# VectorE transposes in an attention and S4 kernel: reciprocals and maxima moved off TensorE, last two units normalised by halves, third quarter of wo moved forward, u times D moved to VectorE

## The chip, the core and the metric

The kernel runs on one core of a Trainium2 chip. The metric is the device time of one launch in microseconds, the median of several executions. Beside the timed runs stands one execution taken by the hardware profiler; every busy time, wait and duration below comes from it. The engines are TensorE (PE, with its weight loads PEld), VectorE (DVE), ScalarE (ACT), GpSimd (POOL) and SyncE (SP). SP here only issues DMAs; GpSimd issues some too.

## The reference

Two independent computations on sequences of 2048 rows, whose results stand side by side in the output (576 columns each). A is sliding-window attention with 32 heads of 18 columns and a window of 256 keys; B is an S4 layer: a convolution over the whole sequence with a kernel computed from the state matrices, plus u times D.

```python
def _A_ref(x, wqkv, wo):
    H = 32; Dh = D // H; W = 256
    qkv = (x @ wqkv).reshape(B, S, 3, H, Dh).transpose(2, 0, 3, 1, 4)
    q, k, v = qkv[0], qkv[1], qkv[2]
    scores = jnp.einsum("bhqd,bhkd->bhqk", q, k) * (Dh ** -0.5)
    mask = (idx[:, None] - idx[None, :] >= 0) & (idx[:, None] - idx[None, :] < W)
    p = _softmax(jnp.where(mask[None, None], scores, -1e9), axis=-1)
    o = jnp.einsum("bhqk,bhkd->bhqd", p, v)
    return o.transpose(0, 2, 1, 3).reshape(B, S, D) @ wo

def _B_ref(u, A_re, A_im, B_re, B_im, C_re, C_im, log_dt, Dskip):
    ...
    K = jnp.einsum("dn,dnl,dn->dl", Cc, P, dB).real
    y = irfft(rfft(pad(u)) * rfft(pad(K)))[:L]
    return y + u * Dskip[None, None, :]
```

## The kernel before

The first half of the launch (to about 513 us) projects x to q, k and v, builds the tables of the S4 kernel and does the first stage of its transforms. The change does not touch it. The second half is `attention`, whose order is written out by hand: every engine works off its instructions in the order in which the program issues them.

Attention is cut into 16 units: unit i = 8 hf + g holds the four heads 4g to 4g + 3 and the 1024 queries of half hf. A unit has six items: two chunks c of 512 queries, each in three banks b of key blocks. The loop over n has 98 rounds; in round n it issues the scores of item n, the products with V of item n - 2, and a share of several generators that `merge` interleaves:

- `gmax` (L629 to L662): for a later unit, the maximum of the scores of every group of 32 queries: 64 products into PSUM, a maximum on VectorE for each 32 queries (L650), a TensorE transpose of the 128 x 32 maxima (L656), a scaling to fp16 (L658), and four DMAs that put them into a row of Q. That row of Q meets rows of K that hold -32768 (L603), so the products of K and Q come with the maxima already subtracted.
- `scores` (L670): products of K and Q (L684), the exponential on ScalarE (L686), mask selections on GpSimd (L695).
- `values` (L698): products with V (L707) into `po`, which collects one chunk; V has a column of ones, so row 18 of each head's 32 rows holds the sum of the exponentials. ScalarE copies `po` to `osb` (L715).
- `norm` (L732), one step a round, for a finished unit: four DMAs bring the sums to `den`, 128 x 32 (L740); reciprocal (L743); VectorE multiplies it with a 0/1 pattern to 128 x 1024 (`spread`, L746); TensorE spreads it over each head's rows with a 0/1 matrix, 512 columns at a time (L755); VectorE multiplies `osb` with that product in PSUM (L756); ScalarE rounds to fp16 (L757), VectorE keeps the rest (L759). Then GpSimd issues four DMAs to `od` in DRAM (L763). Unit 7 stays in SBUF instead (`h7`).
- `norm_last` (L717): unit 15, by chunks: TensorE sums and spreads at once (L721), a reciprocal over 512 columns (L723), the same three steps, into `h7`.
- `conv` (L484): 117 pieces. 32 half steps of three pieces each do the second transform, the product with the kernel's transform and the first inverse (L504, L512, L530 to L541); after 96 pieces and five empty yields 16 output steps follow. Each loads h (SP, four DMAs, L556) and u (GpSimd, four DMAs, L560) two steps ahead, multiplies the next step's u by D on GpSimd (L574), does the last inverse (L578), adds (L581), and SP stores four pieces. Six pieces run before the loop; in the loop `share(n - 2, 111, 96)` spreads 111 over rounds 2 to 97.
- `wo_first` (rounds 62 to 85) and `wo_part` (87 to 96): the products with wo (L901). A group is 128 queries by 288 columns; queries of half 0 (quarters c = 0, 1) are finished in `wo_first`. For half 1, `wo_part` adds up the first half of the rows of wo (k = 0, 1) into SBUF (`acc`). After the loop `wo_operands` loads k = 2, 3 of quarters 2 and 3 from `od` (L889), and `wo_rest` does eight groups of nine products for each quarter and adds `acc` (L935).

Products of `gmax`, `conv`, `norm` and wo share a PSUM ring of three buffers (`ring`); the scores have two of their own, `po` one.

Lines that the steps of the prediction follow in the loop of `attention` before:

```python
k = share(n - 2, 111, 96)
streams.append((part(conv, k), k))
...
if n == 95:
    self.h7[1] = self.p["h7"].tile([128, 2, HQ], F16, name="h7")
    norms.append(self.norm_last(0))
...
for c in (2, 3):
    self.wo_operands(c, 2, 4)
for c in (2, 3):
    for _ in self.wo_rest(c):
        pass
```

## Time and profile before

| | us |
|---|---|
| median of 3 runs | 1113.55 |
| lowest, highest | 1110.69, 1113.61 |
| the profiled execution, its own time | 1108.92 |
| its span in the trace | 1107.2 |
| VectorE, mean of L650 (maximum of 288 columns), x448 in the second half | 0.452 |
| ScalarE, mean of L686 (exponential, 1024 columns) | 1.058 |

How to read the rows that the prediction quotes. A group of instructions has: line, engine, operation, output<-input, shapes, count | busy us in all, mean ns of one | idle us of the engine just before them and what ended it. A row of stretches has: from:to, length, then for PE, PEld, DVE, ACT and POOL busy us (instructions), the TensorE clock that was granted (1.00 is full speed), the mean busy share of the 16 DMA engines, and GB/s. A wait has: who <- for whom: us in total, times, longest. A row of a timeline or of the chain has: start us, us, engine, line, and in brackets the idle time before it. The chain is followed back from the last instruction, at each step to what released it. A row of DMA issues has: output<-input, queue, count, KB each, median us from issue to landing.

### The profile page before, as it was taken

Reading aid. Unit: us, or ns where it says so; the run is one execution under the profiler, and the core shown is the slowest. Engines: PE = TensorE matmul, PEld = TensorE weight load, DVE = VectorE, ACT = ScalarE, POOL = GpSimd, SP = SyncE. Lnnn points to the kernel's source line nnn. Section 1 sums busy time; section 2 is a strip of 40 time slices with the busy share of each in tenths; the row PEclk is TensorE's granted clock in tenths of the full one; section 3 lists DMA queues with packets and bytes.
Section 4 is the critical chain, followed back from the end, with each engine's and each line's share of the span. In section 5 each row is a group of like instructions: output and inputs, shape, how many; then the busy total and the mean of one; then the engine's idle time right before and its main releaser. Section 6 shows DMA issues by size and latency. Waiting matters only on the chain.

```text
span 1107.2 us, 26979 instructions
## 1 busy us (share of the span) xinstructions
PE 891.3 (80%) x10412; PEld 458.8 (41%) x10412; DVE 716.2 (65%) x1805; ACT 622.0 (56%) x955; POOL 532.8 (48%) x618
## 2 busy tenths in 40 slices
PE   1525879897988879975888888889989999998767
PEld 0213436554644554632333333333334444443325
DVE  2879667776775681165767777777777566564363
ACT  1786767776778772232256565565656555554530
POOL 0014335443653360010356776657766665579970
PEclk9557989999998889998899999999999999999998
DMA  9564423443253314698144454644555244376973
GB/s 272 161 194 149 92 58 83 109 103 69 55 130 86 74 47 109 154 266 264 45 119 123 144 160 136 185 99 129 165 156 173 64 146 141 100 188 200 243 193 123
DMA packets 156185, 152.45 MB, mean 138 GB/s; under 512 B 37000, under 2 KB 134664, under 8 KB 155864
## 3 DMA queue, kind: packets, MB, share of 16 engines
q1 hardware_dynamic: 148488, 132.14, 43.4%
q0 software_dynamic: 6064, 14.60, 5.0%
q10 hardware_dynamic: 1504, 3.99, 1.3%
q8 instruction: 82, 1.34, 0.5%
q14 instruction: 47, 0.39, 0.1%
HBM read 89.27 MB, written 61.01 MB: 136 GB/s over the span
## 4 chain that ended last, share of the span: by engine, by line
PE 43%; DVE 20%; DMA 12%; ACT 10%; issue 8%; POOL 5%; SPq 1%; DVEq 0%; ACTq 0%; POOLq 0%
PE pp L176 8%; PE po L707 5%; PE r L901 5%; PE r L643 4%; PE r L504 4%; PE pp L465 3%; PE r L755 3%; PE ST L684 3%; PE r L512 3%; PE kp L422 3%; DMA gk<-g 2%; DVE jk L650 2%; PE x L318 2%; DVE tr L362 2%; POOL P L695 2%
## 5 line engine op out<-in xcount | busy, mean ns | idle before, releaser
L650 DVE CUSTOM_DVE_ANT_0 jk<-r,bias 128x288 f32<-128x288 f32 (+7 forms) x512 | 197.6, 434 | 109.1 <-PE r L643 108.2
L686 ACT ACTIVATE P<-ST,esc 128x1024 f32<-128x1024 f32 (+1 forms) x192 | 201.6, 1058 | 86.9 <-PE ST L684 86.3
L384 POOL TENSOR_TENSOR m<-A,tr 128x1024 f32<-128x1024 f32 x72 | 148.5, 2083 | 193.9 <-PE kp L422 140.3
L695 POOL TENSOR_SCALAR_AFFINE_SELECT P<-P 128x512 f32<-128x512 f32 x240 | 171.4, 743 | 108.2 <-ACT P L686 105.8
L643 PE MATMUL r<-K,qb 128*64 128x288 f16 (+7 forms) x1024 | 128.2, 297 | 17.7 <-DVE t L534 9.3
L707 PE MATMUL po<-P,V 128*32 128x256 f32 (+2 forms) x1408 | 100.6, 397 | 16.5 <-ACT osb L715 6.4
L422 PE MATMUL kp<-Q,m 128*32 128x64 f32 x4608 | 86.4, 227 | 27.2 <-DVE Q L405 11.4
L540 POOL TENSOR_TENSOR Y<-t,t 64x288 f32<-64x288 f32 x64 | 53.9, 842 | 107.6 <-DVE t L535 55.3
L643 PEld LDWEIGHTS <-qb 128*64 128x64 f16 x1024 | 57.3, 109 | 98.2 <-issue 54.8
L422 PEld LDWEIGHTS kp<-Q,m 128*32 128x32 f32 x4608 | 73.5, 114 | 55.4 <-issue 42.4
L465 PE MATMUL pp<-ut,w 128*128 128x288 f32 x128 | 51.1, 524 | 41.8 <-DMA ut<-in_u_dram 24.5
L684 PE MATMUL ST<-Q,K 64*128 64x384 f16 (+2 forms) x704 | 74.2, 282 | 2.3 <-DMA Q<-m 2.1
L241 DVE SCALAR_TENSOR_TENSOR qst<-pp,qst 128x512 f16<-128x512 f32 x36 | 24.7, 686 | 64.1 <-ACT qst L240 64.0
L707 PEld LDWEIGHTS po<-P,V 128*32 128x32 f32 x1408 | 35.9, 110 | 53.7 <-issue 35.6
L541 POOL TENSOR_TENSOR Y<-t,t 64x288 f32<-64x288 f32 x64 | 56.2, 878 | 3.8
L132 ACT ACTIVATE g<-pp 128x288 f32<-128x288 f32 (+1 forms) x84 | 34.4, 447 | 38.1 <-DMA gk<-g 20.5
L465 PEld LDWEIGHTS pp<-ut,w 128*128 128x128 f32 x128 | 27.8, 236 | 61.7 <-issue 18.5
L330 ACT ACTIVATE ab<-k 128x512 f32<-128x512 f32 (+1 forms) x54 | 31.9, 590 | 37.5 <-DVE k L329 37.1
L176 PE MATMUL pp<-xh,wh 128*128 128x512 f16 x180 | 47.6, 386 | 2.7 <-DVE xh L233 1.9
L504 PE MATMUL r<-tx,w 128*64 128x288 f32 x256 | 40.6, 437 | 10.2 <-DMA tx<-gx 9.5
L176 PE MATMUL pp<-xh,wl 128*128 128x512 f16 x180 | 48.5, 394 | 0.0
L176 PEld LDWEIGHTS <-wh 128*128 128x128 f16 x324 | 31.7, 100 | 39.6 <-issue 6.4
(176 smaller groups left out, 1808.6 us busy)
## 6 DMA issues: line engine op xcount, KB each, us to landing
gx<-g SPq DMA_DIRECT2D x32, 288.0 KB
qd<-qst SPq DMA_DIRECT2D x72, 128.0 KB
gk<-g SPq DMA_DIRECT2D x16, 576.0 KB
tx<-gx SPq DMA_DIRECT2D x16, 576.0 KB
tk<-gk SPq DMA_DIRECT2D x16, 576.0 KB
h<-ho SPq DMA_DIRECT2D x16, 576.0 KB
raw<-in_xT_dram SPq DMA_DIRECT2D x16, 512.0 KB
Q<-qd SPq DMA_DIRECT2D x32, 216.0 KB
```

Source lines behind the costliest of these rows:

```text
L176: self.nc.tensor.matmul(ps, u, v, start=(i == 0), stop=(i == len(ops) - 1))
L384: self.nc.gpsimd.tensor_tensor(m, A[:, ch, a0:a0 + 8].unsqueeze(3).to_broadcast(sh), tr[:, ch, part, 0:8].unsqueeze(2).to_broadcast(sh), o ...
L422: nc.tensor.matmul(kp[32 * st:32 * st + 32, c % 2 * JJ2 + j, :], m[:, ch, a0:a0 + 32], Q[:, ch, term % 2, :], start=(term == 0), stop=(ter ...
L465: nc.tensor.matmul(ps, self.w1[:, part, :], src[:, o:o + k], start=True, stop=True)
L504: nc.tensor.matmul(ps[64 * par:64 * par + 64], w2[:, par, 64 * part:64 * part + 64], t[:, 2 * hs:2 * hs + 2, par, :], start=True, stop=True)
L541: nc.gpsimd.tensor_tensor(Y[par][64:128], t1[sl, 1], t2[sl, 1], op=OP.add)
L643: nc.tensor.matmul(ps[64 * b:64 * b + 64, :n], self.qb[:, b, t, :], d["K"][:, b, k0:k0 + n], start=True, stop=True, skip_group_check=True)
L650: nc.vector.tensor_tensor_reduce(out=jk[:, :n], in0=ps[:, :n], in1=self.bias[:, 288 - n:], scale=1.0, scalar=-3e38, op0=OP.add, op1=OP.max ...
L684: nc.tensor.matmul(ps[:, u, o:o + n], d["K"][h, jp, k0:k0 + 128], d["Q"][h, jp, q0:q0 + n], start=True, stop=True, skip_group_check=True)
L686: nc.scalar.activation(pt[:, 2 * jp:2 * jp + 2, lo:hi], ps[:, :, lo:hi], AF.Exp, scale=self.esc)
L695: nc.gpsimd.affine_select(v, v, pattern=[[0, 4], [sg, 128]], compare_op=OP.is_ge, fill=0.0, base=-1 if far else 0, channel_multiplier=-sg)
L707: nc.tensor.matmul(self.po[32 * j:32 * j + 32, t0 * 128:t1 * 128], V[:, kb * 76 + 19 * j:kb * 76 + 19 * j + 32], pt[:, j, o:o + (t1 - t0) ...
```

## The change

- The 0/1 matrices (`c_heads`, L607) go. In `norm`, the reciprocals are transposed on VectorE in blocks of 32 x 32, twice: 128 x 32, and then with each value repeated 32 times to 128 x 1024. That gives the spread reciprocals in SBUF with no TensorE product; VectorE multiplies from SBUF.
- In `gmax`, VectorE scales the maxima and transposes them in blocks of 32 x 32; the four DMAs read the result.
- `norm_last` becomes `norm_chunk` for units 14 and 15, called after each chunk: transpose of 512 columns, reciprocal of the 16 columns that hold the sums, transpose back with repetition, then the same three steps. Unit 14 is written to `od` by halves, eight DMAs of 512 queries for four of 1024.
- The convolution runs 95 of its pieces in rounds 2 to 77 and the last 16, the output steps, in rounds 78 to 94. u times D goes from GpSimd to VectorE.
- The operands of wo for k = 2, 3 of quarters 2 and 3 are loaded in rounds 94 and 96; four of the eight groups of `wo_rest(2)` (the third quarter) stand in round 97.

```diff
@@ conv
             for e in range(qd + (qd > 0), min(qd + 2, 16)):
-                nc.gpsimd.tensor_tensor(nx[e][1], nx[e][1], self.dsk, op=OP.mult)
+                tt(nx[e][1], nx[e][1], self.dsk, op=OP.mult)
@@ att_setup
-        hd = ap.tile([128, 288], F32, name="heads")
-        nc.sync.dma_start(hd, a["c_heads"])
-        self.same, self.pick, self.sums = hd[:, 0:128], hd[:, 128:160], hd[:, 160:288]
@@ gmax
-        mt = self.p["ring"].tile([128, 512], F32, name="r")
-        nc.tensor.transpose(mt[:32, :128], m, self.ident)
-        m16 = self.p["m"].tile([32, 128], F16, name="m16")
-        nc.vector.tensor_scalar(m16, mt[:32, :128], 2.0 ** -15, None, op0=OP.mult)
+        m16 = self.p["m"].tile([128, 32], F16, name="m16")
+        mt = self.p["m"].tile([128, 32], F16, name="mt")
+        nc.vector.tensor_scalar(m16, m, 2.0 ** -15, None, op0=OP.mult)
+        nc.vector.transpose(mt, m16)
         for j in range(4):
             r = 64 * (j % 2) + 54
             self.after(1, nc.sync.dma_start, d["Q"][r:r + 1, j // 2].rearrange("o (s q) -> o s q", q=32),
-                       m16[:, 32 * j:32 * j + 32])
+                       mt[32 * j:32 * j + 32])
@@ norm_last becomes norm_chunk
-        ps = self.p["ring"].tile([128, 512], F32, name="r")
-        nc.tensor.matmul(ps, self.sums, osb[:, cs], start=True, stop=True)
-        rb = self.p["n1"].tile([128, 512], F32, name="rb")
-        nc.vector.reciprocal(rb, ps)
+        rb, den = self.p["n1"].tile([128, 512], F32, name="rb"), self.p["n1"].tile([128, 16], F32, name="denl")
+        nc.vector.transpose(rb, osb[:, cs])
+        nc.vector.reciprocal(den, rb[:, 18::32])
+        nc.vector.transpose(rb, den.unsqueeze(2).to_broadcast([128, 16, 32]))
         yield
...
         nc.vector.tensor_tensor(osb[:, cs], osb[:, cs], rb, op=OP.mult)
         nc.scalar.activation(h[:, 0, cs], osb[:, cs], AF.Copy)
         yield
         nc.vector.tensor_tensor(h[:, 1, cs], osb[:, cs], h[:, 0, cs], op=OP.subtract)
+        yield
+        for j in range(4 if i == 14 else 0):
+            f0 = 72 * 6 + 18 * j
+            nc.gpsimd.dma_start(self.od[:, f0:f0 + 18, HQ + 512 * c:HQ + 512 * c + 512].rearrange("a p n -> p a n"),
+                                h[32 * j:32 * j + 18, :, cs])
         yield
@@ norm
         nc.vector.reciprocal(den, den)
-        X = self.p["n1"].tile([128, 32, 32], F32, name="spread")
-        sh = [128, 32, 32]
-        nc.vector.tensor_tensor(X, den.unsqueeze(1).to_broadcast(sh), self.pick.unsqueeze(2).to_broadcast(sh), op=OP.mult)
+        dt = np_.tile([128, 32], F32, name="dent")
+        nc.vector.transpose(dt, den)
+        X = self.p["n1"].tile([128, HQ], F32, name="spread")
+        nc.vector.transpose(X, dt.unsqueeze(2).to_broadcast([128, 32, 32]))
         yield
...
-            ps = self.p["ring"].tile([128, 512], F32, name="r")
-            nc.tensor.matmul(ps, self.same, X[:, 16 * c:16 * c + 16].rearrange("p s q -> p (s q)"), start=True, stop=True)
-            nc.vector.tensor_tensor(osb[:, cs], osb[:, cs], ps, op=OP.mult)
+            nc.vector.tensor_tensor(osb[:, cs], osb[:, cs], X[:, cs], op=OP.mult)
@@ attention
-                k = share(n - 2, 111, 96)
+                k = share(n - 2, 95, 76) if n < 78 else share(n - 78, 16, 17) if n < 95 else 0
...
+            if n in (94, 96):
+                self.wo_operands(2 + (n - 94) // 2, 2, 4)
...
-            if n == 95:
-                self.h7[1] = self.p["h7"].tile([128, 2, HQ], F16, name="h7")
-                norms.append(self.norm_last(0))
+            if n == 97:
+                streams.append((part(wo2, 4), 4))
             merge(*streams)
             norms = [g for g in norms if next(g, 0) is None]
-            if n >= 2 and (n - 2) % 6 == 5 and n < 97:
+            if n >= 2 and n < 86 and (n - 2) % 6 == 5:
                 norms.append(self.norm(items[n - 2][0]))
                 next(norms[-1])
-        norms.append(self.norm_last(1))
+            elif n >= 86 and (n - 2) % 3 == 2:
+                norms.append(self.norm_chunk(*items[n - 2][:2]))
+                next(norms[-1])
...
-        for _ in wo1:
-            pass
-        for c in (2, 3):
-            self.wo_operands(c, 2, 4)
-        for c in (2, 3):
-            for _ in self.wo_rest(c):
+        for g in (wo1, wo2, self.wo_rest(3)):
+            for _ in g:
                 pass
```

More of the change, by code (lines that the diff above doesn't have):

```diff
@@ L74, in constants @@
     c["c_id"], c["c_bias"] = np.eye(128), bias
-    row = np.zeros((32, 32))
-    row[18] = 1.0
-    c["c_heads"] = np.concatenate([np.kron(np.eye(4), np.ones((32, 32))), np.tile(np.eye(32), (4, 1)),
-                                   np.kron(np.eye(4), row)], axis=1)
     return {k: np.ascontiguousarray(v.astype(ml_dtypes.bfloat16 if k in mult else np.float32)) for k, v in c.items()}
@@ L715, in values, with norm_chunk @@
             nc.scalar.activation(self.osb[i][:, c * 512:c * 512 + 512], self.po, AF.Copy)
-    def norm_last(self, c):
-        nc, osb, cs = self.nc, self.osb[15], slice(c * 512, c * 512 + 512)
-        ps = self.p["ring"].tile([128, 512], F32, name="r")
-        nc.tensor.matmul(ps, self.sums, osb[:, cs], start=True, stop=True)
-        rb = self.p["n1"].tile([128, 512], F32, name="rb")
-        nc.vector.reciprocal(rb, ps)
-        yield
-        h = self.h7[1]
+    def norm_chunk(self, i, c):
+        nc, osb, cs = self.nc, self.osb[i], slice(c * 512, c * 512 + 512)
+        rb, den = self.p["n1"].tile([128, 512], F32, name="rb"), self.p["n1"].tile([128, 16], F32, name="denl")
+        nc.vector.transpose(rb, osb[:, cs])
+        nc.vector.reciprocal(den, rb[:, 18::32])
+        nc.vector.transpose(rb, den.unsqueeze(2).to_broadcast([128, 16, 32]))
+        yield
+        if c == 0:
+            self.hl[i] = self.p["h7"].tile([128, 2, HQ], F16, name="h7") if i == 15 else \
+                self.p["n"].tile([128, 2, HQ], F16, name="oh16")
+        h = self.hl[i]
+        if i == 15:
+            self.h7[1] = h
         nc.vector.tensor_tensor(osb[:, cs], osb[:, cs], rb, op=OP.mult)
@@ L766, in attention @@
     def attention(self, conv):
-        self.V, self.Pt, self.osb, self.ops, norms = {}, {}, {}, {}, []
+        self.V, self.Pt, self.osb, self.ops, self.hl, norms = {}, {}, {}, {}, {}, []
         self.load_unit(0)
@@ L774, in attention @@
         items = [(i, c, b) for i in range(16) for c in range(2) for b in range(3)]
[L775 removed]
+        wo0, wo1, wo2, wl, self.acc, self.h7 = self.wo_first(), self.wo_part(), self.wo_rest(2), self.wo_load(), [], {}
         for n in range(len(items) + 2):
```

1 line of the change is left out of this document (removed).

## The prediction

> **What bounds the kernel now.** I read the busy shares of the whole page first, then the same shares cut into stages, then the groups of instructions in each stage, and last the chain that ended last. Line numbers are those of the kernel before.
>
> ```profile
> span 1107.2 us, 26979 instructions
> PE 891.3 (80%) x10412; PEld 458.8 (41%) x10412; DVE 716.2 (65%) x1805; ACT 622.0 (56%) x955; POOL 532.8 (48%) x618
> ```
>
> TensorE leads, but this is an average over unlike stages. The attention loop starts near 513 us. Item n = 4 ends at 565 us, item 77 near 953 us, and the last product with V near 1072 us.
>
> ```profile
> core 0: us, PE busy (x) PEld busy (x) DVE busy (x) ACT busy (x) POOL busy (x), PEclk, DMA share, GB/s
> 565.10:953.00 387.90, 346.10 (x3126) 153.25 (x3126) 277.30 (x1012) 225.42 (x320) 257.45 (x356) 0.99 0.48 140
> 953.00:1072.40 119.40, 101.64 (x905) 47.20 (x906) 58.95 (x160) 58.06 (x77) 100.26 (x149) 0.97 0.72 198
> 1015.00:1030.00 15.00, 10.80 (x80) 4.25 (x80) 5.29 (x10) 5.86 (x9) 14.66 (x23) 0.89 0.84 228
> 1030.00:1045.00 15.00, 11.52 (x100) 4.92 (x104) 6.52 (x10) 6.59 (x10) 13.47 (x21) 0.96 0.97 254
> ```
>
> In the main stage TensorE is busy 346.1 of 387.9 us (89.2%), VectorE 71%, GpSimd 66%: TensorE sets the pace. In the late stage TensorE is at 85% and GpSimd at 84%; in the two quoted stretches TensorE falls to 72 and 77% while GpSimd is nearly full and the DMA engines reach 0.97.
>
> ```profile
> 1011.45 2.02 POOL L560 DMA_DIRECT2D t<-in_u_dram  x4
> 1013.48 1.41 POOL L574 TENSOR_TENSOR X<-X,dsk 128x576 f32<-128x576 f32 x1
> 1014.83 1.80 POOL L695 TENSOR_SCALAR_AFFINE_SELECT P<-P 128x512 f32<-128x512 f32 x3
> 1016.58 2.00 POOL L560 DMA_DIRECT2D X<-in_u_dram  x4
> DVE t L581 <- DMA out_dram<-t: 29.2, 7, 6.7
> ```
>
> The first four rows are GpSimd's timeline, the last is from the list of waits. GpSimd's queue has no gap: four issues of u, one u times D, three mask selections, 5.1 us a round. VectorE idles 29.2 us until output tiles are stored. The tail, from the chain:
>
> ```profile
> 1070.45 1.00 PE po L707 x16
> 1075.18 1.82 POOL od L763 x3
> 1077.01 3.02 DMA od<-oh
> 1080.43 3.23 DMA ol<-od
> 1083.71 19.81 PE r L901 x142
> 1103.55 0.52 DVE ya L935
> ```
>
> The last product with V ends at T = 1071.45. The rest, 35.75 us, is a chain: normalise, write unit 14, read it back, then the last 142 products with wo.
>
> **The change, main stage (items 4 to 77).** Each of units 0 to 13 had two products spreading the reciprocals, each unit one TensorE transpose of maxima.
>
> ```profile
> L755 PE MATMUL r<-spread,heads 128*128 128x512 f32 x60 | 34.7, 660 | 4.4 <-ACT raw L927 1.2 <-DVE t L536 1.0 <-ACT Y L927 0.6
> L656 PE MATMUL r<-ident,m 128*32 128x128 f32 x16 | 4.6, 288 | 12.4 <-DVE m L650 12.1 <-ACT tk L927 0.3
> 933.27 1.19 PE L504 MATMUL r<-tx,w 128*64 128x288 f32 x8
> 943.36 1.24 PE L512 MATMUL r<-Y,i 128*128 128x288 f32 x4
> DVE jk L650 <- PE r L643: 84.2, 65, 4.0
> ```
>
> The rows are two groups, two stretches of TensorE's timeline, and a wait from the stage up to 953 us. Of the 30 spreading products (two records each) 22 fall here: 22/30 of 34.7 + 4.4 is 28.7 us. Of the 16 transposes 12: 12/16 of 4.6 + 12.4 is 12.8 us, mostly TensorE standing still for the last maximum, which now concerns VectorE alone. Against it stands the new pace of the convolution: 95 pieces by item 77 in place of 87. Five of the eight are empty yields; three are one half step: twice 1.19 us of L504 and 1.24 of L512, 3.6 us. If every microsecond counted, the stage would lose 28.7 + 12.8 - 3.6 = 37.9 us. If TensorE kept its idle share, only removed work would count: (25.4 + 3.5 - 3.6)/0.892 = 28.4 us. I take 28, the lower, since VectorE's share would rise to 277.3/360 = 77%, so its 84.2 us of waiting for TensorE is what shrinks. Ends for the range: 13 (a third of 38) and 38.
>
> What VectorE gets for it:
>
> ```profile
> L746 DVE TENSOR_TENSOR spread<-den,heads 128x1024 f32<-128x1024 f32 x15 | 23.7, 1580 | 0.5
> L743 DVE RECIPROCAL den<-den 128x32 f32<-128x32 f32 x15 | 5.2, 348 | 0.0
> L723 DVE RECIPROCAL rb<-r 128x512 f32<-128x512 f32 x2 | 6.7, 3354 | 0.2 <-PE r L721 0.2
> L166 DVE TENSOR_REDUCE amxo<-raw 128x1 f32<-128x720 f32 x4 | 3.6, 895 | 0.0
> L166 DVE TENSOR_REDUCE amx<-raw 128x1 f32<-128x1280 f32 x8 | 11.6, 1476 | 1.4 <-DMA raw<-in_xT_dram 1.4
> L756 DVE TENSOR_TENSOR osb<-osb,r 128x512 f32<-128x512 f32 x30 | 20.5, 683 | 11.1 <-PE r L755 11.1
> L759 DVE TENSOR_TENSOR oh<-osb,oh 128x512 f16<-128x512 f32 x28 | 28.7, 1025 | 0.0
> ```
>
> The trace has no VectorE transpose. From below: an operation with one source, at (1476 - 895)/560 = 1.04 ns a column, gives 1.21 us for 1024 columns and 0.68 for 512. From above: the reciprocal's 3354/512 = 6.55 ns a column, 6.7 us for 1024. I take the lower, as the reciprocal is the only row so slow and a transpose computes nothing. So the 1024-column transpose replaces a 1.58 us multiply, and the small transposes (32 columns, at most the reciprocal's 0.35 us) cost about the difference. At the upper end 14 units would add 72 us to an engine with 111 us spare in this stage; at a quarter landing that is 18 us lost. [...]
>
> The multiply L756 read one operand from PSUM (683 ns); it now reads both from SBUF, as L759 does, whose mean is 1025 ns. That is 28 x 0.34 = 9.6 us more on VectorE, and u times D adds such instructions in the late stage. I charge 2 us of the end for both: most of it falls into VectorE's idle time. Ends: 0 and 10.
> [...]
>
> Before item 4 two more transposes leave the start: 1 us.
>
> **Late stage (items 78 to 97).** Sixteen output steps of the convolution ran beside items 84 to 97 and now run beside 78 to 94; u times D moves to VectorE.
>
> ```profile
> L574 POOL TENSOR_TENSOR X<-X,dsk 128x576 f32<-128x576 f32 x8 | 11.9, 1490 | 0.4 <-DMA X<-in_u_dram 0.3
> L574 POOL TENSOR_TENSOR t<-t,dsk 128x576 f32<-128x576 f32 x8 | 11.7, 1460 | 1.8 <-DMA t<-in_u_dram 1.7
> L763 POOL DMA_DIRECT2D od<-oh x56 | 33.4, 599 | 3.9 <-DVE oh L759 3.9
> X<-in_u_dram POOLq DMA_DIRECT2D x32, 72.0 KB, 4.2
> DVE t L581 <- DMA t<-in_u_dram: 6.3, 1, 6.3
> ```
>
> Floors, worked out for each engine. GpSimd: 100.3 - 23.6 (u times D) + 8 x 0.6 (unit 14 written in halves: eight issues, formerly four after T) = 81.5 us. TensorE: 101.6 - 9.3 (8 of 30 spreading products) - 1.0 (one product of the last norm) - 0.6 - 3.6 = 87 us. DMA: 0.72 x 119.4 = 86 us of full load; the four operand loads (1.0 MB) and unit 14's writes (0.6 MB) were after T and add 1.6/23.6 of it, 92 us. So GpSimd stops being the bound and the DMA engines take over. They held 0.97 for 15 us (quoted); at that the stage takes 95 us, at 0.87 it takes 106. I take 106, a gain of 13; ends 0 and 25.
>
> The moved loads sit in SP's queue at items 94 and 96, where each waits for unit 14's halves; behind them stand the output stores of the last two steps and one of wo, whose buffers nobody claims soon: nothing. The new wait is u times D on VectorE: it needs the u of the next step, issued an item (about 5 us) earlier and landing 4.2 us after issue. Behind it on VectorE stand the step's own additions, which free two of three ring buffers for TensorE, and the norm pieces. I cost it at nothing while an item lasts longer than issue and landing.
>
> **Tail.** In the changed program four of the sixteen last groups stand right behind the final product with V, four behind them, then the eight of the last quarter.
>
> ```profile
> 864.24 1.84 PE r L901 x15
> L757 ACT ACTIVATE oh<-osb 128x512 f16<-128x512 f32 x28 | 17.7, 631 | 52.1 <-DVE osb L756 52.1
> ```
>
> A group of nine takes 9 x 1.84/15 = 1.10 us. TensorE: four groups to T + 4.4. VectorE clears these first (0.52 each), to T + 5.0, then normalises the last half: two transposes of 512 columns (0.68 each), a reciprocal of 16 (0.25, by the slope from 32 to 512 columns), multiply 0.69, ScalarE's copy 0.63, subtract 0.69: 3.6 us, with handovers T + 8.8. Meanwhile three more groups fill the ring's three buffers; the eighth waits for VectorE until T + 9.3. Nine groups from there: T + 19.2. From the last product to the end of the span it is 1107.2 - 1103.5 = 3.7, as before. T + 22.9 against T + 35.75 saves 12.8 us; with the slow transpose (3.35 each) 7.5.
>
> **Sum.** 28 + 13 + 12.8 + 1 - 2 = 52.8. The profiled execution took 1108.92 us (span 1107.2), so 1056. The median of the three runs, 1113.55, lies 4.6 above it; with about 4 the forecast is 1060 us.
>
> **Rivals.** (B) All of it lands: the ring, rid of 46 tiles, lets TensorE run ahead. 38 + 25 + 12.8 + 1 = 76.8: 1036. For: TensorE waited 12.4 us at the transposes alone. Against: the DMA share it needs.
> [...]
> (D) Slower: each u times D stops VectorE, in order, until u has landed; ring buffers stay full and TensorE and its followers stop. At the full landing time 16 x 4.2 = 67 us lost in place of 13 won: 1108.9 - 39.8 + 67 = 1136, with the 4 1140. It decides from 39.8/16 = 2.5 us a step. For: the 6.3 us row. Against: that wait came once, with GpSimd issuing late.
> (E) The third quarter is not beside anything: unit 14's halves come back late and the sixteen groups start at T + 8, 17.6 us and 3.7 to the end: 6.4 us saved, not 12.8: 1066.
>
> **Chances.** Forecast 0.53, B 0.18, C 0.14, E 0.08, D 0.07. The range runs from B to just above C, 1036 to 1092; the forecast's own is 1045 to 1075. Below 0.3% this kernel cannot be told from no change: faster 0.90 (all but D and 0.03 of C, whose spread reaches back to the old time), same 0.02 and slower 0.08.
>
> **What would show it.** Main: time between the copies of the V products falls from 15.9 us (387.9 us over 73 items) to about 14.8 us per three items, VectorE above 75%. Transpose of 1024 columns near 1.2 us; 3 us or more refutes that price. Late: GpSimd gaps appear, DMA share above 0.85; a VectorE wait for u in more than half of the steps would speak for D. Tail: last product with V to the end about 23 us, with one pause of TensorE near 2 us. Wrong altogether if the main stage still takes over 380 us.

## The result, and the profile after

The changed kernel takes 1077.67 us, the median of four runs (1075.61 to 1079.41), beside 1113.58 us for the kernel before: a ratio of 0.9681, 95% interval 0.9655 to 0.9706. The forecast was 1060 us, with a range from 1036 to 1092 and a range of its own from 1045 to 1075. So the time is in the wide range, 2.7 us above the narrow one, and nearer to the wide range's upper end (14.3 us) than to the forecast (17.7 us). The profiled execution of the changed kernel took 1075.61 us, its span 1073.6.

I divided both launches at the copies of `po` to `osb`, of which there are 32, one for each chunk: the main stage runs from the first to the 25th (rounds 4 to 76), the late stage from there to the 32nd, the tail from there to the end of the span. These borders lie near the prediction's, a few us apart at the stage ends.

| stage | before | after | gain | forecast |
|---|---|---|---|---|
| up to the first copy | 565.1 | 566.1 | -1.0 | 1 |
| main | 383.1 | 369.4 | 13.7 | 28 |
| late | 124.3 | 114.7 | 9.5 | 13 |
| tail | 34.8 | 23.4 | 11.4 | 12.8 |
| charge for the slower multiplies | | | | -2 |
| span | 1107.2 | 1073.6 | 33.6 | 52.8 |

Counted from the last product with V, as the prediction counts it, the tail went from 35.75 to 23.5 us, 12.3 of the 12.8 that were forecast. In the kernel before, the last copy starts 1.0 us behind that product, as ScalarE has two other instructions to do first; the table puts this microsecond into the late stage.

Nearly all that lies ahead of the first copy is the same program in every kernel of this study, and that copy falls anywhere from 564.05 to 571.5 us: a microsecond in that row tells nothing. In the main stage, four kernels that hold the same program there (after, u4, u5 and e6 below) give 369.3 to 370.3 us. Each stage is read from one profiled execution, though: that of the kernel before is 4.7 us faster than the median of its kernel, that of the changed kernel 2.1.

The first line of the page after, then both stages before and after (from:to, length, busy us and instructions of PE, PEld, DVE, ACT, POOL, granted clock, DMA share, GB/s):

```profile
PE 857.8 (80%) x10332; PEld 450.7 (42%) x10332; DVE 736.2 (69%) x1859; ACT 619.9 (58%) x955; POOL 511.1 (48%) x606
```
```profile
565.10:948.18 383.08, 341.95 (x3088) 151.40 (x3088) 273.09 (x997) 221.88 (x315) 255.25 (x354) 0.99 0.49 141
948.18:1072.45 124.27, 105.84 (x946) 49.09 (x946) 63.21 (x176) 61.64 (x84) 102.46 (x151) 0.97 0.70 190
```
```profile
566.08:935.46 369.38, 320.84 (x3056) 145.41 (x3056) 288.53 (x1024) 221.91 (x321) 257.83 (x363) 1.00 0.53 151
935.46:1050.19 114.73, 93.76 (x909) 45.18 (x908) 73.45 (x204) 59.07 (x77) 79.48 (x135) 0.96 0.77 205
```

In the main stage TensorE is busy 341.95 - 320.84 = 21.1 us less, but its idle time rose from 41.1 to 48.5 us, and 21.1 - 7.4 makes the 13.7. The forecast had 25.3 us less work and let the idle time shrink by 3 us with it. VectorE went from 71 to 78% of the stage. In the late stage GpSimd fell from 82 to 69%, to 79.5 us of work, near its floor of 81.5.

What TensorE waited for in the main stage, before and then after:

```profile
PE r L656 <- DVE m L650: 9.7, 12, 0.8
PE r L512 <- DVE m L650: 1.8, 5, 0.6
PE r L504 <- DVE m L650: 1.7, 2, 1.3
```
```profile
PE r L636 <- DVE qb L627: 9.9, 9, 1.6
PE r L500 <- DVE m L643: 5.8, 10, 1.9
PE r L508 <- DVE m L643: 4.4, 8, 0.9
```

The 9.7 us that TensorE stood at the transpose of the maxima did not go away. It moved one step on: to `qb`, the copy of the next unit's queries, which stands behind the last maximum, the scaling and the new transpose in VectorE's order. The waits for a maximum that frees a ring buffer tripled, from 3.5 to 10.2 us.

VectorE's groups over the launch (mean ns after the bar):

```profile
L751 DVE STREAM_TRANSPOSE spread<-dent 128x1024 f32<-128x1024 f32 x14 | 17.4, 1245 | 0.5
L715 DVE STREAM_TRANSPOSE rb<-osb 128x512 f32<-128x512 f32 x4 | 2.8, 698 | 2.8 <-ACT osb L708 2.8
L759 DVE TENSOR_TENSOR osb<-osb,spread 128x512 f32<-128x512 f32 x28 | 28.9, 1031 | 0.0
L627 DVE COPY qb<-Q 54x2048 f16<-54x2048 f16 x32 | 30.8, 962 | 0.5
```

The transposes cost 1245 and 698 ns for 1024 and 512 columns (forecast 1.21 and 0.68 us), the multiply from SBUF 1031 ns (forecast 1025). The copy to `qb`, which the change does not touch, went from 829 ns to 962.

The tail, from the chain:

```profile
1050.12 4.54 PE r L903 x36
1054.69 0.52 DVE ya L937
1055.21 0.63 DVE rb L715
1055.86 0.27 DVE denl L716
1056.15 0.72 DVE rb L717
1056.90 0.70 DVE osb L725
1057.62 0.64 ACT h L726
1058.89 0.52 DVE ya L937
1059.46 10.13 PE r L903 x81
```

The last product with V ends at T = 1050.12. Four groups of TensorE stand on the chain; three more run beside the normalising and are not on it; then comes one pause of TensorE (1.49 us), nine groups, and the end at T + 23.5: step for step as worked out (T + 22.9).

### The profile page after: what moved, and what is told of

It reads as the page before. It is cut to its first block, busy times and chain, and to the rows that moved or that the text cites. A ratio compares the mean times of both kernels' runs of the same rounds, so it can differ in the third digit from the quotient of the medians.

```text
span 1073.6 us, 26801 instructions
## 1 busy us (share of the span) xinstructions
PE 857.8 (80%) x10332; PEld 450.7 (42%) x10332; DVE 736.2 (69%) x1859; ACT 619.9 (58%) x955; POOL 511.1 (48%) x606
## 4 chain that ended last, share of the span: by engine, by line
PE 37%; DVE 25%; ACT 10%; DMA 10%; issue 9%; POOL 5%; SPq 2%; DVEq 0%; ACTq 0%; POOLq 0%
PE pp L172 8%; PE r L636 4%; PE po L700 4%; PE r L903 4%; PE r L500 4%; PE kp L418 4%; PE pp L461 3%; DVE jk L643 3%; POOL P L688 2%; DMA gk<-g 2%; PE ST L677 2%; PE x L314 2%; PE r L508 2%; DVE tr L358 2%; ACT P L679 2%
## 5 line engine op out<-in xcount | busy, mean ns | idle before, releaser
L636 PE MATMUL r<-K,qb 128*64 128x288 f16 (+7 forms) x1024 | 130.5, 297 | 36.7 <-DVE qb L627 10.7
L700 PE MATMUL po<-P,V 128*32 128x256 f32 (+2 forms) x1408 | 100.2, 395 | 17.5 <-POOL P L688 8.1
L636 PEld LDWEIGHTS <-qb 128*64 128x64 f16 x1024 | 60.3, 109 | 119.3 <-issue 65.6
L461 PE MATMUL pp<-ut,w 128*128 128x288 f32 x128 | 52.8, 538 | 40.9 <-DMA ut<-in_u_dram 18.6
L700 PEld LDWEIGHTS po<-P,V 128*32 128x32 f32 x1408 | 35.7, 110 | 52.5 <-issue 25.7
L500 PE MATMUL r<-tx,w 128*64 128x288 f32 x256 | 40.2, 430 | 9.9 <-DMA tx<-gx 8.7
```

What stands on the lines that cost most here:

```text
L461: nc.tensor.matmul(ps, self.w1[:, part, :], src[:, o:o + k], start=True, stop=True)
L500: nc.tensor.matmul(ps[64 * par:64 * par + 64], w2[:, par, 64 * part:64 * part + 64], t[:, 2 * hs:2 * hs + 2, par, :], start=True, stop=True)
L636: nc.tensor.matmul(ps[64 * b:64 * b + 64, :n], self.qb[:, b, t, :], d["K"][:, b, k0:k0 + n], start=True, stop=True, skip_group_check=True)
L700: nc.tensor.matmul(self.po[32 * j:32 * j + 32, t0 * 128:t1 * 128], V[:, kb * 76 + 19 * j:kb * 76 + 19 * j + 32], pt[:, j, o:o + (t1 - t0) ...
```

## The experiments

All ratios are to the kernel before, with 95% intervals; stages as above, from the profiled execution of each. "After" stands first, kernels that undo or alter one part follow.

| kernel | median | ratio | main | late | tail |
|---|---|---|---|---|---|
| after | 1077.67 | 0.9681 [0.9655, 0.9706] | 369.4 | 114.7 | 23.4 |
| u1_old_pace | 1086.43 | 0.9769 [0.9737, 0.9801] | 368.9 | 116.4 | 30.6 |
| u2_maxima_tensore | 1085.85 | 0.9759 [0.9719, 0.9799] | 375.0 | 115.3 | 23.4 |
| u3_norm_tensore | 1096.76 | 0.9864 [0.9815, 0.9914] | 388.7 | 116.2 | 23.3 |
| u4_ud_gpsimd | 1078.48 | 0.9698 [0.9662, 0.9734] | 369.3 | 117.5 | 23.4 |
| u5_quarter_after | 1078.35 | 0.9700 [0.9664, 0.9735] | 370.3 | 114.7 | 23.5 |
| b1_pace_alone | 1113.63 | 1.0015 [0.9994, 1.0036] | 395.9 | 117.7 | 32.1 |
| e6_ud_late | 1076.02 | 0.9669 [0.9645, 0.9693] | 370.2 | 114.1 | 23.4 |
| e7_qb_first | 1106.68 | 0.9947 [0.9927, 0.9966] | 393.8 | 115.3 | 23.4 |
| e8_rest_gpsimd | 1070.12 | 0.9608 [0.9577, 0.9639] | 361.3 | 116.7 | 23.4 |
| d1_transpose_twice | 1092.53 | 0.9829 [0.9796, 0.9863] | 379.0 | 118.5 | 23.4 |
| e9_qb_first_blank | 1112.29 | 1.0010 [0.9986, 1.0034] | 403.8 | 117.0 | 23.1 |
| e10_both | 1064.25 | 0.9576 [0.9534, 0.9619] | 359.1 | 113.8 | 23.4 |

### One part undone: pace, maxima, norm, u times D

u1_old_pace, the change with the old pace of the convolution:

```diff
-                k = share(n - 2, 95, 76) if n < 78 else share(n - 78, 16, 17) if n < 95 else 0
+                k = share(n - 2, 111, 96)
```

> The changed kernel with the old pace of the convolution: 111 pieces over rounds 2 to 97. Main stage means from the first copy of the products with V (round 4) to the 25th (round 76): 383.1 us before, 369.4 after. Theory W (VectorE has become the late one in the main stage; the pace costs only the work of the moved half steps): main stage 363 to 367 us, late stage and tail longer by more than that, 1080 to 1088 us in all. Rival P (the pace is what ate the main stage's gain: eight more pieces crowd the ring): main stage 352 to 358 us, and the time about the same as after, 1072 to 1079.

u2_maxima_tensore, the maxima transposed on TensorE as before:

```diff
-        m16 = self.p["m"].tile([128, 32], F16, name="m16")
-        mt = self.p["m"].tile([128, 32], F16, name="mt")
-        nc.vector.tensor_scalar(m16, m, 2.0 ** -15, None, op0=OP.mult)
-        nc.vector.transpose(mt, m16)
+        mt = self.p["ring"].tile([128, 512], F32, name="r")
+        nc.tensor.transpose(mt[:32, :128], m, self.ident)
+        m16 = self.p["m"].tile([32, 128], F16, name="m16")
+        nc.vector.tensor_scalar(m16, mt[:32, :128], 2.0 ** -15, None, op0=OP.mult)
```

> The changed kernel with the maxima transposed on TensorE again. The prediction's price for this part was 12.8 us in the main stage and 1 before it: it would be back, 1089 to 1092 us. Theory W says that TensorE's wait for the last maximum did not go but moved to the next unit's qb copy (9.7 us of waiting before, 9.9 us after): removing the transposes gained no more than their 3.5 us of work and VectorE paid 5 us more for scaling and transposing: 1074 to 1081 us, with the wait for qb under 3 us and that for the last maximum near 10.

u3_norm_tensore, the reciprocals of units 0 to 13 spread by TensorE as before:

```diff
...
-        nc.vector.transpose(X, dt.unsqueeze(2).to_broadcast([128, 32, 32]))
+        nc.vector.tensor_tensor(X, den.unsqueeze(1).to_broadcast(sh), self.pick.unsqueeze(2).to_broadcast(sh), op=OP.mult)
...
-            nc.vector.tensor_tensor(osb[:, cs], osb[:, cs], X[:, cs], op=OP.mult)
+            nc.tensor.matmul(ps, self.same, X[:, 16 * c:16 * c + 16].rearrange("p s q -> p (s q)"), start=True, stop=True)
+            nc.vector.tensor_tensor(osb[:, cs], osb[:, cs], ps, op=OP.mult)
```

> The changed kernel with the reciprocals of units 0 to 13 spread by TensorE again (pattern multiply, 0/1 matrix, osb times PSUM). By the prediction's price (28.7 us in the main stage, 6 to 8 in the late one, two thirds landing or more) 1100 to 1112 us. Theory W: VectorE gets back 8 us of slower multiplies, so the part was worth 10 to 18 us: 1088 to 1096 us.

u4_ud_gpsimd, u times D on GpSimd as before:

```diff
-                tt(nx[e][1], nx[e][1], self.dsk, op=OP.mult)
+                nc.gpsimd.tensor_tensor(nx[e][1], nx[e][1], self.dsk, op=OP.mult)
```

> The changed kernel with u times D on GpSimd again. If GpSimd was the bound of the late stage and the move freed it (prediction): late stage (25th to 32nd copy, 114.7 us after) 122 to 130 us, 1085 to 1093 us in all. Rival: VectorE's 23 us of waiting for u (8 of 16 steps) cost what GpSimd gained: late stage 111 to 118, 1073 to 1081 us.

The old pace costs the changed kernel nothing in the main stage (368.9 against 369.4) and 7.2 us in the tail, where the last output steps then stand among the products with wo. VectorE in the tail of u1_old_pace:

```profile
1061.80 0.82 DVE L577 TENSOR_TENSOR t<-r,t 128x288 f32<-128x288 f32 x2 [3.88 <-DMA out_dram<-t]
1064.86 0.70 DVE L715 STREAM_TRANSPOSE rb<-osb 128x512 f32<-128x512 f32 x1
```

An output step waits 3.88 us for a store, and the last norm stands behind it. With the maxima on TensorE the main stage grows by 5.6 us; the wait at the transpose is back with 9.9 us in 12 waits, and the one for `qb` is gone. With the norm on TensorE it grows by 19.3. Moving u times D is worth nothing that these runs can tell, as the rival had it; GpSimd is back at 86% of the late stage, the stage differs by 2.8 us, and the intervals of the two ratios overlap.

Not all of what was expected came out. For u1_old_pace the time is Theory W's (1080 to 1088), but the main stage lies above its range, and far above that of Rival P, which is refuted. The time of u2_maxima_tensore, 1085.85, lies between its two expectations; 4.6 us of its launch stand ahead of the first copy, where a difference tells nothing, so the 5.6 of the main stage is the better price. The time of u3_norm_tensore, 1096.76, is just above Theory W's range and below the price of the prediction.

### The third quarter of wo

u5_quarter_after:

```diff
-            if n in (94, 96):
-                self.wo_operands(2 + (n - 94) // 2, 2, 4)
...
-            if n == 97:
-                streams.append((part(wo2, 4), 4))
...
-        for g in (wo1, wo2, self.wo_rest(3)):
-            for _ in g:
-                pass
+        for _ in wo1:
+            pass
+        for c in (2, 3):
+            self.wo_operands(c, 2, 4)
+        for g in (wo2, self.wo_rest(3)):
+            for _ in g:
+                pass
```

> The changed kernel with the operands of wo for quarters 2 and 3 loaded behind the loop and no group of the third quarter in the last round. Theory (the third quarter only fills the time of the last norm): the loads land about 3.5 to 4 us after T, when the last half is normalised, and sixteen groups of 1.10 us and the 3.7 us to the end give T + 25 to T + 27 in place of T + 23.5; the late stage stays at 113 to 115 us; worth 2 to 3 us in all. Rival E of the prediction, read from the other side (without this part the groups start at T + 8): T + 29. Rival F (the four loads in the late stage load the DMA engines, which bound it: 1.0 of 23.6 MB): the late stage falls by 3 to 4 us and the whole is the same.

All three missed: stages and time are those of the changed kernel. The late stage is no shorter, and the tail no longer. TensorE at the end of the last product with V in u5_quarter_after:

```profile
1050.29 0.72 PE L700 MATMUL po<-P,V 128*32 128x384 f32 x12
1050.94 0.30 PE L903 MATMUL r<-woh,oh 126*128 126x288 f16 x1
```

The first product with the operands in question starts without a pause, so they had landed: SP issues the loads from 1045.4 to 1050.4, before T (1051.0 here), though they stand behind the loop. With unit 14 written in halves, this edit does nothing; the groups beside the last norm are there in this kernel too.

### The pace alone

b1_pace_alone is the kernel before with the new pace and nothing else:

```diff
-                k = share(n - 2, 111, 96)
+                k = share(n - 2, 95, 76) if n < 78 else share(n - 78, 16, 17) if n < 95 else 0
```

> The kernel before with the new pace of the convolution alone (95 pieces by round 77, the last 16 by round 94). Undoing the norm part alone cost 19.3 us of main stage and the maxima alone 5.6, together 24.9, but before and after differ there by 13.7 only. If the pace costs the main stage 11 us as long as TensorE still spreads and transposes (the crowded ring), main stage 390 to 396 us and the whole 1104 to 1112, the tail some 7 us shorter. If the pace is free in the main stage and the two parts simply do not add, main stage 382 to 386 us and the whole 1096 to 1104.

In all it is neutral, but not by stage: the main stage grows by 12.8 us, and late stage and tail give back 6.6 and 2.6. So the first expectation holds in the main stage (390 to 396 us), but not for the tail, which was to be 7 us shorter, nor for the whole (1104 to 1112). The main stage of this kernel, and TensorE's timeline behind one of its waits:

```profile
567.81:963.67 395.86, 352.15 (x3112) 154.68 (x3112) 273.42 (x1001) 224.61 (x321) 262.59 (x364) 0.97 0.48 140
```
```profile
660.56 1.45 PE L707 MATMUL po<-P,V 128*32 128x384 f32 x8 [1.51 <-POOL P L695]
661.94 2.19 PE L504 MATMUL r<-tx,w 128*64 128x288 f32 x8
667.93 1.19 PE L504 MATMUL r<-tk,w 128*64 128x288 f32 x8
```

TensorE is busy 10.2 us longer than before, for 3.6 us of added work (the prediction's estimate); the mean clock is 0.97 in place of 0.99. The clock records of the two traces have 27.3 us of this stage at a granted clock of 0.50, against 10.2 before. Behind a wait of 1.51 us the eight products of L504 take 2.19 us, six us later again 1.19. Why the new pace makes TensorE wait longer for GpSimd's masks in this kernel (7.3 us in the stage, 2.6 before) is not shown. Nor is all of the 12.8 us certain: the two profiled executions differ by 6.3 us in span, the medians of the two kernels hardly at all.

With u1_old_pace this makes a square of main stages:

| | old pace | new pace |
|---|---|---|
| old norm and maxima | 383.1 | 395.9 |
| new norm and maxima (with the rest of the change) | 368.9 | 369.4 |

At the new pace, norm and maxima gain 26.5 us, near the forecast's 28; at the old pace they gain 14.2. The parts do not add. The ratios, from more executions, say the same of the whole launch: without the pace the change gains 2.3% (u1), on top of it 3.3% (b1 to after), some 11.5 us apart.

### Is VectorE now a bound of the main stage?

e8_rest_gpsimd takes the subtraction that keeps the rest of the fp16 rounding (L762) off VectorE in units 0 to 13, to GpSimd; d1_transpose_twice gives VectorE more, by doing each 1024-column transpose twice:

```diff
-            nc.vector.tensor_tensor(h[:, 1, cs], osb[:, cs], h[:, 0, cs], op=OP.subtract)
+            nc.gpsimd.tensor_tensor(h[:, 1, cs], osb[:, cs], h[:, 0, cs], op=OP.subtract)
```
```diff
         nc.vector.transpose(X, dt.unsqueeze(2).to_broadcast([128, 32, 32]))
+        nc.vector.transpose(X, dt.unsqueeze(2).to_broadcast([128, 32, 32]))
```

> The changed kernel with the rest (osb minus its fp16 rounding, L762) of units 0 to 13 on GpSimd: VectorE loses 18 us of 288 in the main stage, GpSimd gains some 30 of 258. Theory W (VectorE shares the bound of the main stage): main stage 355 to 364 us, 1064 to 1073. If TensorE alone is the bound, or GpSimd gives it back: main stage 367 to 373, 1075 to 1085.

> The changed kernel with the 1024-column transpose of units 0 to 13 done twice into the same tile (the values do not change): 12 more of 1.245 us in the main stage, 14.9 us more on VectorE, nothing on any other engine. Theory W (VectorE shares the main stage's bound): by the rate that e8_rest_gpsimd gave, 8.1 us of the stage for 21.4 us taken off VectorE, 0.38 a microsecond, the stage grows by 5.7, to 372 to 379 us, and the ratio to before is about 0.974. Rival I (the 80 us that VectorE is idle there hide it; e8 gained by other means): 368 to 371 us, ratio 0.966 to 0.970. Rival L (TensorE and VectorE in lockstep, each microsecond counts): 384 us, ratio 0.981.

The main stage of e8_rest_gpsimd, and in it the subtraction on GpSimd and the multiply before it on VectorE:

```profile
566.89:928.20 361.31, 320.21 (x3056) 147.16 (x3056) 267.09 (x1002) 222.06 (x321) 276.38 (x385) 0.99 0.53 154
```
```profile
L762 POOL TENSOR_TENSOR oh<-osb,oh 128x512 f16<-128x512 f32 x20 | 23.2, 1158 | 0.0
L759 DVE TENSOR_TENSOR osb<-osb,spread 128x512 f32<-128x512 f32 x22 | 18.2, 828 | 0.0
```

VectorE has 21.4 us less, the stage 8.1, TensorE's work is the same. The subtraction is dearer on GpSimd (1158 ns, 821 on VectorE in this stage), and still the trade wins; the multiply fell from 1066 to 828 ns. The other way, eleven of the second transposes (13.7 us) fall into the stage, and VectorE is busy 12.2 us longer in all. The stage of d1_transpose_twice and TensorE's first wait in it:

```profile
565.29:944.32 379.03, 321.64 (x3056) 144.97 (x3056) 300.71 (x1035) 221.88 (x321) 258.26 (x362) 1.00 0.51 146
```
```profile
PE r L500 <- DVE m L643: 12.4, 17, 1.9
```

The stage grows by 9.6 us, 0.8 for each microsecond of the 12.2: the upper end of Theory W, short of the 384 of Rival L, the lockstep. The ratio speaks for Rival L: its 0.981 lies in the interval, 0.9796 to 0.9863, and Theory W's 0.974 does not. The profiled execution was the fastest of six, 4.3 us under their median. So between 0.8 and the whole of each added microsecond counts, and these runs do not decide where. Rival I, that VectorE's idle time hides it, is refuted from both sides. The extra wait is where the change had put one already: TensorE at L500, for a maximum that frees a ring buffer, 5.8 to 12.4 us.

### The copy of the next unit's queries

e7_qb_first puts that copy ahead of the scaling and transposing of the finished unit's maxima:

```diff
+                    ng = self.gmax(i + 2)
+                    next(ng)
                     next(gm, 0)
                     next(gm, 0)
-                    gm = self.gmax(i + 2)
+                    gm = ng
```

> The changed kernel with the next unit's qb copy ahead of the scaling and transposing of the maxima on VectorE. Theory W: TensorE's wait for qb (9.9 us) shrinks by about 0.6 us in each of 12 units, main stage 361 to 365 us, 1070 to 1074. If the wait only moves on to the ring: main stage 368 to 371, 1076 to 1080.

Both theories missed: it is 29 us slower, 24.4 of them in the main stage. Its longest wait there, the stage itself, TensorE's timeline around one of those waits, and the two stretches behind it:

```profile
PE r L636 <- DVE qb L627: 26.1, 12, 3.0
```
```profile
571.48:965.27 393.79, 332.26 (x3058) 149.11 (x3056) 284.95 (x1026) 222.11 (x322) 256.14 (x364) 0.95 0.49 140
```
```profile
747.85 0.61 PE L677 MATMUL ST<-Q,K 64*128 64x384 f16 x8
751.44 0.69 PE L636 MATMUL r<-K,qb 128*64 128x288 f16 x4 [2.98 <-DVE qb L627]
752.06 1.08 PE L700 MATMUL po<-P,V 128*32 128x256 f32 x8
753.08 2.29 PE L508 MATMUL r<-Y,i 128*128 128x288 f32 x4
```
```profile
752.00:755.00 3.00, 3.00 (x14) 1.38 (x12) 1.02 (x6) 0.41 (x1) 2.93 (x6) 0.50 0.03 2
755.00:758.00 3.00, 3.00 (x25) 0.92 (x28) 0.96 (x5) 2.46 (x4) 2.09 (x5) 0.60 0.48 102
```

The copy was a step of its own in the interleaving. With that step gone, the first products that need `qb` come earlier in the round than before: here straight behind the scores, ahead of the products with V (L700) and the convolution (L508), where in the changed kernel other products stand in between:

```profile
642.66 0.64 PE L700 MATMUL po<-P,V 128*32 128x256 f32 x8
643.23 1.19 PE L500 MATMUL r<-tx,w 128*64 128x288 f32 x8
644.36 0.39 PE L677 MATMUL ST<-Q,K 64*128 64x128 f16 x4
645.52 0.25 PE L636 MATMUL r<-K,qb 128*64 128x32 f16 x4 [0.78 <-DVE qb L627]
```

So TensorE gets there before the copy: in five of the twelve units it waits 2.98 us, in seven 1.6. After the long waits it comes back at about half speed: here the four products of L508 take 2.29 us, elsewhere in this kernel 1.21. Of the 24.4 us that the stage lost, 13.0 are idle time and 11.4 are longer products.

e9_qb_first_blank was to keep the products in place (against e7_qb_first):

```diff
-                    gm = ng
+                    gm = (next(ng, 0) if s else None for s in range(99))
```

> The changed kernel with the next unit's copy of Q (qb) put ahead of the scaling and transposing of the maxima, as in e7_qb_first, but with an empty step left where the copy stood in the interleaving, so that every pair of products keeps its place in the round. Theory W (VectorE's order delays TensorE at the unit's end; e7 lost because its first pair of products moved forward in the round): TensorE's wait for qb falls from 9.9 us to 0 to 4 us, the main stage from 369.4 to 361 to 366 us, ratio to before 0.960 to 0.967. Rival (the late maxima themselves hurt, since the rows of Q that they fill come later): the main stage is again above 380 us, as the 393.8 of e7, and the ratio above 0.98. Third case: the wait goes and the stage stays at 368 to 371 us; then the wait for qb was not on the path.

It does not test what it was meant to: the name `ng` is looked up late, so the next unit's first two steps are taken by the two calls that should finish the last one, and two pairs of products are issued right behind the copy, at the head of the round. The scaling and transposing of the last unit's maxima then stand ahead of the copy again (at 648.05 and 648.70 us, the copy at 648.83), and one unit's are left out altogether: 15 transposes of maxima in place of 16. So the run matches its rival's numbers without testing the rival. What it does show is the cost of two pairs of products close behind the copy, where e7 has one: the wait for `qb` 30.6 us in 12 waits, the longest 4.0, main stage 403.8.

e10_both has the step in the right place (against e8_rest_gpsimd):

```diff
+                    ng = self.gmax(i + 2)
+                    next(ng)
                     next(gm, 0)
                     next(gm, 0)
-                    gm = self.gmax(i + 2)
+                    gm = (next(o, 0) if s else None for o, s in zip([ng] * 99, range(99)))
```

> e8_rest_gpsimd with the next unit's copy of Q (qb) ahead of the scaling and transposing of the maxima, and an empty step left in its place, so that TensorE's order is that of e8 word for word and on VectorE only these two steps change places. (In e9_qb_first_blank the empty step was passed to the wrong unit: its first two pairs of products were issued right behind the copy, ahead of the round's scores and products with V. It tells only what the copy costs with still more products close behind it.) Theory W: the wait for qb, 9.9 us in the changed kernel, falls to 0 to 4 us and the main stage from 361.3 to 352 to 358 us, ratio to before 0.950 to 0.957. Rival 1 (the copy was not on the path, another wait takes its place): main stage 359 to 363 us, ratio 0.958 to 0.964. Rival 2 (maxima that come later hold up the scores): main stage above 366 us, ratio above 0.966.

Waits of TensorE in the main stage, e8_rest_gpsimd and then e10_both:

```profile
PE r L636 <- DVE qb L627: 9.3, 9, 1.6
PE po L700 <- POOL P L688: 4.2, 7, 0.9
```
```profile
PE po L700 <- POOL P L688: 8.0, 10, 1.5
PE r L636 <- DVE qb L627: 0.9, 3, 0.5
```

Rival 1: the wait for `qb` is gone (9.3 to 0.9 us), but the stage gains 2.2 us, since TensorE now reaches the products with V before GpSimd has masked P. The copy itself, put first with the products kept in their places, costs nothing here, so what e7 lost it lost by the missing step, as far as a kernel that also carries e8's edit can tell. e10_both is the fastest kernel of the study, 13 us under the changed one; its step over e8 alone, 0.9608 to 0.9576, is within the intervals.

### u times D a step later

e6_ud_late puts each u times D behind its step's additions:

```diff
-            for e in range(qd + (qd > 0), min(qd + 2, 16)):
-                tt(nx[e][1], nx[e][1], self.dsk, op=OP.mult)
+            if qd == 0:
+                tt(ut, ut, self.dsk, op=OP.mult)
...
             yield
+            if qd < 15:
+                tt(nx[qd + 1][1], nx[qd + 1][1], self.dsk, op=OP.mult)
```

> The changed kernel with each u times D one output step later, just ahead of the addition that needs it, so that u has an item more to land. If VectorE's wait for u (23 us, 8 steps of 16) delays TensorE through the ring: wait under 6 us, late stage 108 to 112 us (114.7 after), 1071 to 1075 us. If the DMA engines set the pace of the late stage: the wait goes over to h or to the output stores, late stage 113 to 117, 1076 to 1080 us.

VectorE's waits for DMAs of the output steps, after and then e6_ud_late:

```profile
DVE X L570 <- DMA X<-in_u_dram: 16.0, 5, 5.4
DVE t L570 <- DMA t<-in_u_dram: 7.0, 3, 4.1
DVE t L577 <- DMA out_dram<-t: 4.2, 2, 2.3
```
```profile
DVE t L577 <- DMA out_dram<-t: 17.4, 4, 6.6
DVE t L580 <- DMA t<-in_u_dram: 1.3, 1, 1.3
```

23.0 us of waiting for u become 1.3, and 13.2 us more turn up as waiting for the stores; late stage and time stay as they are, as the second expectation had it.

## Why the prediction was right, and where it was wrong

The time lies in the stated range, 17.7 us above the forecast. No error hid another: every large term came out below its forecast, and the main stage alone makes 14 of the 19 us by which the sum was too large.

**Tail: right in its steps.** T + 23.5 where T + 22.9 was worked out, the same single pause. Rival E's condition, halves of unit 14 that come back late, did not arise. But the credit was misplaced: that the third quarter stands in the loop did nothing (u5), and 7 us of the tail hang on the pace (u1), a gain that the prediction did not name: it counted the tail from T as if no output step stood behind T.

**Prices: right, and GpSimd pays as well.** The transposes of 1024 and 512 columns are within 5% of the lower bound (1245 ns for 1.21 us, 668 to 712 ns for 0.68); the upper (6.7 us for 1024 columns) is refuted. The multiply's mean rose from 683 to 1031 ns, and the last section shows where: in the changed kernel 1117 to 1292 ns where it began during GpSimd's work, 680 to 689 where it did not. GpSimd lost too: in the main stage 17 mask selections began during such a multiply and took 970 to 1087 ns, against a median of 637, some 6.5 us more in all. Yet the mean of all 178 selections of the stage stayed (746 ns before, 744 after). Before, selections were longer beside the multiply to 128 x 1024 that the change removes: the seven that began during it took 1515 to 1661 ns, against a median of 634. The prediction counted no such relief. What these longer instructions cost the stage was not tried apart.

**Main stage: wrong size, 28 forecast, 13.7 measured.** The step that failed is "if TensorE kept its idle share, only removed work would count". The removed work was near (25.3 forecast, 21.1 found), but the idle share rose from 10.7 to 13.1%. The reason given for a steady share, that VectorE's 84.2 us of waiting for TensorE would shrink, looks at the stage as an average. That waiting did shrink (81.0 to 69.3 us between the copies), but at the end of each unit VectorE is the later one, and there the change gave it more to do. The transpose's 12.8 us, called "mostly TensorE standing still", were worth 5.6 (u2), because the standing still went over to the copy of the next unit; the spreading products' 28.7 were worth 19.3 (u3). e8 and d1 show VectorE as a second bound, at 0.4 to 0.8 us of the stage, or more, for each us of its work; taken off it (e10), the stage falls to 359.1, a gain of 24.0 of the 28.
In this stage the lower end of the range, 13, was the better number. That VectorE holds TensorE is shown by the waits (9.9 us for `qb`, 10.2 for maxima that free a ring buffer). GpSimd's single selections were longer beside VectorE's multiplies (970 to 1087 ns), but its work in the stage hardly grew (255.3 to 257.8 us), so that is not what gave the gain back.

**The pace: priced at 3.6 us, which is right for neither kernel.** With the old norm it costs up to 12.8 (b1), with the new one nothing (u1). Whichever way one goes through the square, the whole is 13.7; a sum of separately priced parts cannot give it.

**Late stage: 13 forecast, 9.5 measured.** GpSimd's share fell as said, but that it had been the bound is not borne out: moving u times D, the largest term of its floor, gained nothing measurable in the changed program (u4). The DMA engines work at 0.77 of full load over the stage, not the 0.87 that was taken. The new pace alone shortens the stage by 6.6 us (b1), the change without it by 7.9 (u1); what bounds the stage stays open. Rival D's mechanism came true in form, a wait for u in 8 of 16 steps, but 23.0 us in all are 1.4 a step, under the 2.5 from which it decides, and they took the place of waits for stores (29.2 us before, 4.2 after), which the forecast had not followed: e6 turns them back into those.

## What to carry to other kernels

When a wait is removed from the leading engine, look at what stands next in the order of the engine that it waited for: here 9.7 us at the transpose of the maxima became 9.9 us at the copy to `qb`. In the main stage of the changed kernel VectorE, busy 78%, held TensorE, busy 87%, and it showed in waits by place, not in shares; take something off such an engine and add something to it, and see whether the stage follows (8.1 us of the stage for 21.4 taken off in e8, 9.6 for 12.2 added in d1). When an instruction is moved in a hand-interleaved order, check what its own step had kept apart: in e7, products that came some 2 us earlier in the queue cost 24.4 us of the main stage, where 9.9 us of waiting were to be saved.

## What the runs showed of the hardware

In e7_qb_first a short wait of TensorE cost more than its length. In the main stage each of the five waits of 2.98 us went with a stretch at a granted clock of 0.50, of 6.8 us in four cases and 3.4 in one; a four-product group in such a stretch took 2.29 us for 1.21. In all, 37.5 us of that stage ran at 0.50, against 3.4 in the changed kernel. The length of the wait does not settle whether such a stretch follows. In b1_pace_alone all six waits of 1.28 to 1.51 us were followed by one within 2 us. Longer ones were not always: six of the seven waits of 1.59 to 1.60 us in e7_qb_first, and all three of 1.58 to 1.59 in the changed kernel, were followed by products at full speed. What decides between them stays open.

With both inputs in SBUF, VectorE's multiply of 512 columns took 679 to 692 ns in some places and up to 1292 ns in others. Two groups of the changed kernel, of the same size and both with two inputs in SBUF (ns min/median/max, then first and last start):

```profile
L759 DVE TENSOR_TENSOR osb<-osb,spread x28: 680/1120/1292, 598.7 to 1024.4; 128x512 f32<-128x512 f32 x28
L725 DVE TENSOR_TENSOR osb<-osb,rb x4: 679/686/692, 1019.4 to 1056.9; 128x512 f32<-128x512 f32 x4
```

Set beside GpSimd's timeline, the first group falls into two. The 19 multiplies that began while a mask selection or a convolution product of GpSimd was running took 1117 to 1292 ns; the nine that began while it was idle took 680 to 689. The four of the second group met no computing instruction of GpSimd. Before, with one input in PSUM, all 30 took 673 to 690 ns, though 28 of them began during such work of GpSimd. In e8_rest_gpsimd only six of the 28 took over 690 ns, which is why the mean fell (828 ns in the main stage). There, five that began during a convolution product of GpSimd kept to 685 to 687 ns, so the start alone does not decide it. The copy to `qb` shows the same: 643 to 691 ns in the four cases that met nothing on GpSimd, 867 to 1192 in the other 28.
